# Two weights staged in spare activation buffers and narrowed earlier, and one matmul group moved ahead of another

## The chip, the cores and the metric

One core of a Trainium2 chip runs the whole program in one launch. The metric is the device time of one execution in microseconds (us). Before the change three runs gave 575.04, 575.33 and 576.16 us: a median of 575.33 us.

## What is computed

Three layers follow each other for a batch of 4 sequences of 576 positions. The first is attention with 8 heads of 64, a window of 128 and a linear bias. Its output, 512 wide, is the x of a gated layer:

```
h = gelu(x @ w_in)                       # 512 -> 1024
u, v = h[..., :512], h[..., 512:]
v_n = (v - mean(v)) / sqrt(var(v) + 1e-6) * g_ln
v_s = einsum('ts,bsd->btd', w_sg, v_n) + b_sg[None, :, None]     # w_sg is 576 x 576
y = x + (u * v_s) @ w_out                # w_out is 512 x 512
```

The third layer takes y through a second pair of weights with a convolution over positions and a gate. The weights w_in, w_out and those of the third layer arrive as 64-bit floats; w_sg arrives as 32-bit floats.

## The kernel before, in words

Every product is made from two-part operands: a value is split into a rounded part ("hi") and the rest ("lo"), and the three products hi\*hi, hi\*lo and lo\*hi are added up in PSUM (`mm`, L207). A 64-bit weight is first narrowed to 32 bits by five VectorE instructions (`narrowed`, L287: L301, L303, L304, L305, L306), then split by a copy (L216 on ScalarE or L219 on GpSimd) and a subtraction (L225).

The order of the work is written out as a list of steps (`_steps`, L55). A letter names the work, and the numbers say batch, half of the sequence and tile. Those that matter here, for batch 0:

- `V0.j` (`m_v`, L697): the psv product for positions j\*128 on, 12 matmuls, then gelu on ScalarE, statistics on VectorE, a power on GpSimd, a scaling and a split into vn. There are five.
- `U0.half.m` (`m_u`, L730): the psu product, 12 matmuls, and its gelu on ScalarE.
- `G0.half.m` (`m_sg`, L767): the pss product of w_sg and vn, 14 matmuls, read out by VectorE at L783. Its last two matmuls take the fifth piece of w_sg and the fifth vn.
- `W0.half.m` (`m_wo`, L788): the pso product with w_out, read out by VectorE into x.
- `L`, `M`, `C`, `E`, `N`, `T`, `A` for the next batch's attention: loads, scores with nine masking instructions on VectorE (L426), exponentials on ScalarE, scaling, transposes, and the product with the values.
- `g0` to `g4` (`w_sg_piece`, L343): one 128-row piece of w_sg is loaded, copied into its hi part and subtracted into its lo part.
- `ok.h` (`w_out_piece`, L349): one of eight pieces of w_out (128 rows by 256 columns) is loaded, narrowed and split.

The list is a priority and not the final order: a scheduler that runs at build time lays each engine's instructions in one fixed sequence. It takes the ready instruction that stands first in the list, by a timing model of its own, and it assigns buffers as they come free. `tc.keep_in_program_order` pins an instruction behind the one written just before it on the same engine. `later` (L326) keeps a load behind the last load of w_in on the queue of SyncE (SP), which issues nearly all loads.

Three sets of buffers matter. Tag "st" has four (`NST`): the keys and queries of a batch use them (`a_load`, L380), and before the change the pieces of w_sg and w_out too. Tag "x" has eight: batch 0 holds four of them for its attention output, and the other four are first wanted by batch 1. Tag "v" has three (`NV`): the v of a `V` step and the narrowed piece of w_out share them. The products psv, psu, pss and pso share two PSUM banks (`gps`).

The room in which the hi and lo parts of w_sg and w_out are kept holds inputs of batch 0's attention first (`z_room`, L567), so nothing can be written there until that attention is over.

Of the kernel before, what the change touches and what calls it, by code (L numbers as in the profile page):

```python
# [7 lines left out]
F32 = mybir.dt.float32  # L8
F32R = mybir.dt.float32r
# [30 lines left out]
SLACK = 6000.0  # L40

ON = {
    "clamp": "dve", "win hi": "act", "win lo": "pool", "w64 hi": "pool", "w64 lo": "pool", "w32 hi": "act pool", "w32 lo": "dve",
    "norm": "dve pool",
    "x hi": "act pool", "x lo": "dve", "x first hi": "act", "x first lo": "pool", "x late hi": "act", "x late lo": "dve", "vn first hi": "act", "vn first lo": "dve", "vn hi": "pool", "vn lo": "dve",
    "gate": "pool", "g hi": "act dve pool", "g lo": "dve pool", "x2 hi": "act pool", "x2 lo": "dve",
# [8 lines left out]
def _steps():  # L55


    def of(p):
        return f"{p // NP}.{p % NP}"

    def scores(p):
        return [f"C{of(p)}"]

    def weigh(p):
        return [f"E{of(p)}", f"N{of(p)}"]

# [12 lines left out]
    put_by = [f"a{i}.{c}" for i in (1, 0) for c in range(16)]
    s = """  # L80
        l0.0 k0 l1.0 k5 l2.0 l3.0 v0.0 v1.0 v2.0 v3.0 j1.0 j1.1 l0.1
        c0.0 e0.0 c1.0 e1.0 n0.0 c2.0 e2.0 t0.0 n1.0 c3.0 e3.0 l1.1 j1.2 j1.3 v0.1 i1.0 z0.0 X0.0.0 t1.0 n2.0 z1.0 X0.1.0
        l2.1 v1.1 i1.1 t2.0 n3.0 z2.0 X0.2.0 c0.1 e0.1 l3.1 j0.0 i1.2 t3.0 z3.0 X0.3.0 c1.1 e1.1 v2.1 i1.3 n0.1 c2.1 e2.1 j0.1 v3.1 j0.2 t0.1 n1.1 z0.1
        i0.0 c3.1 e3.1 j0.3 k4 V0.0 t1.1 n2.1 z1.1 i0.1 V0.1 t2.1 n3.1 z2.1 i0.2 U0.0.0 t3.1 z3.1 X0.0.1 U0.0.1
        X0.1.1 i0.3 U0.0.2 X0.2.1 X0.3.1 U0.0.3
    """.split()
    for b in range(B - 1):
        p = NP * (b + 1)
        V = [f"V{b}.{j}" for j in range(5)]
        U = [[f"U{b}.{half}.{m}" for m in range(4)] for half in range(2)]  # L90
        G = [[f"G{b}.{half}.{m}" for m in range(4)] for half in range(2)]
        W = [[f"W{b}.{half}.{m}" for m in range(4)] for half in range(2)]
        if b == 0:
            uv = V[2:4] + loads(p) + scores(p) + V[4:] + loads(p + 1) + U[1][:2] + scores(p + 1) + loads(p + 2) + U[1][2:] + scores(p + 2)
        else:
            uv = V[:2] + loads(p) + scores(p) + V[2:] + loads(p + 1) + scores(p + 1) + U[0] + loads(p + 2) + U[1][:1] + scores(p + 2) + U[1][1:]
        T, A = ([f"{x}{of(p + i)}" for i in range(4)] for x in "TA")
        gw = weigh(p) + G[0] + weigh(p + 1) + G[1][:1] + loads(p + 3) + T[:1] + W[0][:1] + A[:1] + halves(p)
        gw += weigh(p + 2) + W[0][1:2] + T[1:2] + W[0][2:] + A[1:2] + scores(p + 3) + halves(p + 1) + weigh(p + 3) + G[1][1:2] + T[2:3] + G[1][2:3]
        gw += A[2:3] + halves(p + 2) + G[1][3:] + T[3:] + W[1][:1] + A[3:] + halves(p + 3) + W[1][1:]  # L100
        if b == 0:
            s += weave(uv, [f"g{c}" for c in range(5)] + [f"o{k}.0" for k in range(4)]) + ["o0.1"] + gw[:2] + ["o1.1"] + gw[2:4] + ["o2.1"] + gw[4:6] + ["o3.1"] + gw[6:]
        else:
            now = put_by[10 * b - 10 : 10 * b]
            s += weave(uv, now[:4]) + weave(gw, now[4:])
    first = " ".join(s)
    n = [f"V3.{j}" for j in range(5)] + [f"U3.{half}.{m}" for half in range(2) for m in range(4)]
    n += [f"G3.0.{m}" for m in range(4)] + ["G3.1.0"] + [f"W3.0.{m}" for m in range(4)]
    n += [f"G3.1.{m}" for m in range(1, 4)] + [f"W3.1.{m}" for m in range(4)]

    for m in range(4):
        n[n.index(f"U3.{m % 2}.{m // 2 + 1}")] += f" w0.{m // 2}.{m % 2}"
    n[n.index("W3.0.3")] += " y0.0"
    n[n.index("G3.1.2")] += " y0.1"
# [20 lines left out]
def attention_gmlp_glu_kernel(  # L135
# [24 lines left out]
    def f(ap):  # L160
        return ap.bitcast(F32)
# [148 lines left out]
    def prep64(hi, lo, src, n, pool, tag, bufs, spool, stag, sbufs):  # L310
        a = narrowed(src, n, pool, tag, bufs, spool, stag, sbufs)
        split(hi, lo, a, "w64")

    def prep32(hi, lo, src, n, pool, tag, bufs):
        st = pool.tile([P, S], F32, tag=tag, name="wst", bufs=bufs)
        later(nc.sync.dma_start(st[:, :n], src))
        tc.keep_in_program_order(copy(hi, st[:, :n], engines=ON["w32 hi"]))
        tt(lo, st[:, :n], f(hi), ALU.subtract, ON["w32 lo"])
# [16 lines left out]
    def w_in_piece(half, k):  # L335
# [3 lines left out]
        else:  # L339
            sl = slice(k * P, (k + 1) * P)  # L340
            split(winh[:, :, sl], winl[:, :, sl], a.rearrange("p (k n) -> p k n", k=NK), "win")

    def w_sg_piece(c):  # L343
        if c == 0:
            kept["wsg"] = [w1pool.tile([P, 5, S], F32R, tag=f"wsg{i}", name=f"wsg{i}") for i in range(2)]
        wsg = kept["wsg"]
        prep32(wsg[0][:, c, :], wsg[1][:, c, :], w_sg[:, c, :], S, apool, "st", NST)

    def w_out_piece(k, half):  # L349
        if k == half == 0:  # L350
            kept["wo"] = [w1pool.tile([P, NK, DM], F32R, tag=f"wo{i}", name=f"wo{i}") for i in range(2)]
        wo = kept["wo"]
        sl = slice(half * 256, (half + 1) * 256)
        prep64(wo[0][:, k, sl], wo[1][:, k, sl], cols(w_out, k, half * 256, 256), 256, mpool, "v", NV, apool, "st", NST)

    p2pool = []

# [209 lines left out]
    def z_room(i):  # L567

        if i not in room:
            tag, n = (("wsg0", 5 * S), ("wsg1", 5 * S), ("wo0", NK * DM), ("wo1", NK * DM))[i]  # L570
            room[i] = w1pool.tile([P, n], F32, tag=tag, name="zin")
        return room[i]

# [214 lines left out]
    def m_wo(b, half, m):  # L788
        sl = HALF[half]
        n = sl.stop - sl.start  # L790
        cm = slice(m * P, (m + 1) * P)
        ps = gps.tile([P, 512], F32, tag="g", name="pso")
        o = ps[:, :n]
        wo = kept["wo"]
        i = 0
        for k in range(NK):
            hi, lo = gts[b, k, half]
            for w, a in ((wo[0], hi), (wo[1], hi), (wo[0], lo)):
                mm(o, w[:, k, cm], a, start=i == 0, stop=i == 3 * NK - 1)
# [249 lines left out]
```

## Time and profile before

| | us |
|---|---|
| median of three runs | 575.33 |
| the profiled execution | 575.59 |
| its span, first to last instruction | 573.7 |
| TensorE busy | 535.0 |
| VectorE busy | 381.1 |
| GpSimd busy | 266.3 |
| ScalarE busy | 246.3 |

The span is what the trace covers; 1.9 us of the profiled execution lie around it. Mean granted clock of TensorE was 0.979 of 2.4 GHz. The engines are named PE (TensorE), PEld (its weight loads), DVE (VectorE), ACT (ScalarE), POOL (GpSimd) and SP (the loads' queue). L207 is line 207 of the kernel. A square bracket in a timeline row gives the engine's idle time just before the row, and what ended it.

### The profile page before, as it was taken

Reading aid. Unit: us, or ns where it says so; the run is one execution under the profiler, and the core shown is the slowest. Engines: PE = TensorE matmul, PEld = TensorE weight load, DVE = VectorE, ACT = ScalarE, POOL = GpSimd, SP = SyncE. Lnnn points to the kernel's source line nnn. Section 1 sums busy time; section 2 is a strip of 40 time slices with the busy share of each in tenths; the row PEclk is TensorE's granted clock in tenths of the full one; section 3 lists DMA queues with packets and bytes.
Section 4 is the critical chain, followed back from the end, with each engine's and each line's share of the span. In section 5 each row is a group of like instructions: output and inputs, shape, how many; then the busy total and the mean of one; then the engine's idle time right before and its main releaser. Section 6 shows DMA issues by size and latency. Waiting matters only on the chain. (4 is left out here: it accounts for less than half of the span.)

```text
span 573.7 us, 11857 instructions
## 1 busy us (share of the span) xinstructions
PE 535.0 (93%) x4496; PEld 481.9 (84%) x4496; DVE 381.1 (66%) x974; ACT 246.3 (43%) x635; POOL 266.3 (46%) x410
## 2 busy tenths in 40 slices
PE   7867897899999899998999999998999999999997
PEld 6656687798789798888998889996898999898887
DVE  5978389964795886868876887678766533654300
ACT  6785147452328452239443311244545333434301
POOL 3653127931235362325362454468696354455500
PEclk9898897999999899999999999999999999999999
DMA  8971053443161457250735334630201210100011
GB/s 303 353 257 40 5 183 111 145 152 122 45 186 50 153 179 221 75 162 2 218 107 167 109 95 133 211 151 11 91 20 47 91 38 19 39 19 20 37 38 55
DMA packets 33208, 63.91 MB, mean 111 GB/s; under 512 B 3968, under 2 KB 13952, under 8 KB 33152
## 3 DMA queue, kind: packets, MB, share of 16 engines
q1 hardware_dynamic: 33008, 63.04, 33.2%
q8 instruction: 35, 0.57, 0.4%
q14 instruction: 21, 0.17, 0.1%
q10 hardware_dynamic: 144, 0.13, 0.1%
HBM read 48.47 MB, written 14.68 MB: 110 GB/s over the span
## 5 line engine op out<-in xcount | busy, mean ns | idle before, releaser
L207 PE MATMUL psg<-x2g,w 128*128 128x288 f32 x768 | 107.0, 296 | 1.2 <-DVE x2g L225 1.2
L207 PEld LDWEIGHTS psg<-x2g,w 128*128 128x128 f32 x768 | 104.5, 188 | 3.6 <-DVE x2g L225 2.1
L207 PE MATMUL psg<-wout,gh 128*128 128x512 f32 (+1 forms) x272 | 81.2, 383 | 1.8 <-ACT gh L216 1.8
L181 ACT ACTIVATE t<-t,st 128x192 f32<-128x192 f32 (+1 forms) x144 | 61.8, 432 | 21.4 <-DVE st L426 21.4
L207 PE MATMUL pss<-wsg,vn 128*128 128x256 f32 (+1 forms) x448 | 66.2, 306 | 3.6 <-DVE t L783 3.4
L207 PEld LDWEIGHTS pss<-wsg,vn 128*128 128x128 f32 x448 | 62.8, 197 | 4.6 <-DVE t L783 4.6
L207 PE MATMUL psu<-xh,win 128*128 128x256 f32 (+1 forms) x256 | 54.6, 306 | 8.1 <-ACT win L216 3.7
L909 DVE SCALAR_TENSOR_TENSOR cc<-hb,cw,cc 128x576 f32<-128x576 f32 x32 | 29.0, 908 | 49.1 <-POOL cc L236 49.1
L207 PEld LDWEIGHTS psg<-wout,gh 128*128 128x128 f32 x272 | 49.5, 188 | 12.2 <-ACT gh L216 2.4
L207 PE MATMUL pso<-gh,wo 128*128 128x256 f32 (+1 forms) x256 | 52.8, 301 | 3.0 <-DVE x L225 2.2
L207 PE MATMUL psv<-win,xh 128*128 128x512 f32 (+1 forms) x160 | 52.8, 410 | 2.7 <-ACT win L216 1.3
L207 PE MATMUL psg<-wout,gl 128*128 128x512 f32 (+1 forms) x136 | 52.1, 384 | 0.4 <-POOL gl L225 0.3
L236 POOL TENSOR_SCALAR t<-t,r 128x192 f32<-128x192 f32 (+1 forms) x86 | 40.5, 487 | 24.6 <-PE o L207 5.3
L207 PEld LDWEIGHTS psu<-xh,win 128*128 128x128 f32 x256 | 42.4, 193 | 10.1 <-ACT win L216 4.2
L225 POOL TENSOR_TENSOR gl<-gg,gh 128x512 fp32r<-128x512 f32 x32 | 46.7, 1459 | 1.0 <-ACT gh L216 1.0
L236 POOL TENSOR_SCALAR cc<-hb,cw 128x576 f32<-128x576 f32 x32 | 27.5, 862 | 39.8 <-ACT hb L905 39.8
L426 DVE CUSTOM_DVE_ANT_0 t<-sc,tab 128x192 f32<-128x192 f32 (+1 forms) x144 | 40.2, 335 | 6.4 <-PE sc L207 6.2
L207 PEld LDWEIGHTS pso<-gh,wo 128*128 128x128 f32 x256 | 40.2, 188 | 4.8 <-DVE x L225 2.7
L905 ACT ACTIVATE hb<-psg 128x576 f32<-128x576 f32 x32 | 20.7, 653 | 52.9 <-PE psg L207 51.4
L225 DVE TENSOR_TENSOR gg<-cc,hb 128x576 f32<-128x576 f32 x32 | 30.3, 952 | 18.0 <-ACT cc L181 17.6
L207 PE MATMUL pso<-gl,wo 128*128 128x256 f32 (+1 forms) x128 | 37.5, 301 | 3.9 <-DVE gl L225 3.9
L225 POOL TENSOR_TENSOR t<-t,u 128x256 f32<-128x256 f32 (+1 forms) x32 | 27.1, 852 | 28.1 <-DVE t L783 20.6
(89 smaller groups left out, 1048.7 us busy)
## 6 DMA issues: line engine op xcount, KB each, us to landing
V<-in_v_dram SPq DMA_DIRECT2D x12, 704.0 KB, 4.6
w<-in_w_out_dram SPq DMA_DIRECT2D x24, 256.0 KB, 3.0
x2s<-x2d SPq DMA_DIRECT2D x16, 288.0 KB, 3.0
w<-in_w_in_dram SPq DMA_DIRECT2D x8, 512.0 KB, 6.2
w<-in_w_in_dram SPq DMA_DIRECT2D x16, 256.0 KB, 2.8
wout<-w2d SPq DMA_DIRECT2D x8, 512.0 KB, 5.7
q<-in_q_dram SPq DMA_DIRECT2D x12, 320.0 KB, 3.8
out_dram<-ot SPq DMA_DIRECT2D x15, 256.0 KB, 2.0
```

Source lines behind the costliest of these rows:

```text
L181: ins = nc.scalar.activation(*args, **kw)
L207: return nc.tensor.matmul(out, lhsT, rhs, start=start, stop=stop, **kw)
L225: return (nc.vector if eng == "dve" else nc.gpsimd).tensor_tensor(dst, a, b, op=op)
L236: e.tensor_scalar(dst, src, col, 1.0, op0=ALU.mult, op1=ALU.mult)
L426: nc.vector.tensor_tensor_reduce(e, bank, table, scale=-SCALE, scalar=3e38, op0=ALU.add, op1=ALU.min, accum_out=mx)
L905: nc.scalar.activation(h[:, 1 : S + 1].rearrange("p (a n) -> p a n", a=2), ps[:, :, :288], AF.Relu)
L909: nc.vector.scalar_tensor_tensor(cc, h[:, 0:S], cw[:, 0, c : c + 1], cc, op0=ALU.mult, op1=ALU.add)
```

## The change

1. `w_sg` and `w_out` pieces are loaded into buffers of tag "x" and no longer into tag "st" (`staged` replaces the loads in `prep32` and `prep64`).
2. The steps `g` and `o` stand elsewhere in the list. Before, the `g` pieces and `o0.0` to `o3.0` were spread evenly over the work from `V0.2` to the third scores of batch 1, and `o0.1` to `o3.1` stood among the `G0` steps. Now all thirteen stand before the first `G0` step.
3. `V0.2` stands before `U0.0.3` and no longer behind it.
4. The copy into the hi part of a w_sg piece is no longer pinned. The hi copy of w_out goes to ScalarE (was GpSimd); the subtraction stays on GpSimd.
5. The hi and lo parts of w_out lie in one tile and no longer in two. Its size is that of the two together.

```diff
-        X0.1.1 i0.3 U0.0.2 X0.2.1 X0.3.1 U0.0.3
+        X0.1.1 i0.3 U0.0.2 X0.2.1 X0.3.1
...
-            uv = V[2:4] + loads(p) + scores(p) + V[4:] + loads(p + 1) + U[1][:2] + scores(p + 1) + loads(p + 2) + U[1][2:] + scores(p + 2)
+            uv = ["g0", V[2], "o0.0", U[0][3], "g1", "o0.1", V[3]] + loads(p) + ["o1.0"] + scores(p) + ["o1.1", V[4], "o2.0", "g2", "o2.1"]
+            uv += loads(p + 1) + U[1][:2] + ["g3", "o3.0"] + scores(p + 1) + ["g4", "o3.1"] + loads(p + 2) + U[1][2:] + scores(p + 2)
...
-            s += weave(uv, [f"g{c}" for c in range(5)] + [f"o{k}.0" for k in range(4)]) + ["o0.1"] + gw[:2] + ["o1.1"] + gw[2:4] + ["o2.1"] + gw[4:6] + ["o3.1"] + gw[6:]
+            s += uv + gw
...
+    def staged(src, dtype):
+        st = mpool.tile([P, S], dtype, tag="x", name="wst", bufs=8)[:, : src.shape[-1]]
+        later(nc.sync.dma_start(st, src))
+        return st
...
-        prep32(wsg[0][:, c, :], wsg[1][:, c, :], w_sg[:, c, :], S, apool, "st", NST)
+        hi, lo = (w[:, c, :] for w in kept["wsg"])
+        st = staged(w_sg[:, c, :], F32)
+        copy(hi, st, engines=ON["w32 hi"])
+        tt(lo, st, f(hi), ALU.subtract, ON["w32 lo"])
...
-        prep64(wo[0][:, k, sl], wo[1][:, k, sl], cols(w_out, k, half * 256, 256), 256, mpool, "v", NV, apool, "st", NST)
+        st = staged(cols(w_out, k, half * 256, 256), U32)
+        a = narrowed(st, 256, mpool, "v", NV, None, "x", 8)
+        split(kept["wo"][:, k, half, 0, :], kept["wo"][:, k, half, 1, :], a, "wo")
```

`ON["wo hi"]` is ScalarE and `ON["wo lo"]` GpSimd. `m_wo` and `z_room` address the one tile in place of the two.

## Rows read from the trace of the kernel before

**Rows 1.** The page: busy time by engine, and the masking group of VectorE.

```profile
PE 535.0 (93%) x4496; PEld 481.9 (84%) x4496; DVE 381.1 (66%) x974; ACT 246.3 (43%) x635; POOL 266.3 (46%) x410
...
L426 DVE CUSTOM_DVE_ANT_0 t<-sc,tab 128x192 f32<-128x192 f32 (+1 forms) x144 | 40.2, 335 | 6.4 <-PE sc L207 6.2
```

**Rows 2.** Stretches: length, busy PE, PEld, DVE, ACT, POOL (count), PEclk, DMA share, GB/s.

```profile
59.00:63.00 4.00, 4.00 (x12) 3.20 (x13) 0.00 (x0) 0.00 (x0) 1.17 (x1) 0.59 0.00 0
63.00:69.00 6.00, 5.47 (x46) 4.39 (x48) 1.43 (x3) 1.36 (x3) 0.74 (x2) 1.00 0.01 4
69.00:83.00 14.00, 13.41 (x145) 11.87 (x136) 12.41 (x49) 4.19 (x10) 4.07 (x8) 1.00 0.46 144
...
94.00:100.40 6.40, 6.40 (x28) 6.40 (x29) 5.65 (x14) 3.04 (x14) 6.40 (x12) 0.54 0.26 84
100.40:113.00 12.60, 11.85 (x194) 10.65 (x191) 12.43 (x27) 6.74 (x17) 12.60 (x22) 1.00 0.36 117
...
140.50:218.00 77.50, 74.15 (x768) 67.80 (x768) 58.88 (x200) 35.53 (x115) 30.50 (x57) 0.98 0.42 128
```

**Rows 3.** Who PE waited for from 57 to 140.5 us: total, times, longest.

```profile
PE pss L207 <- DVE t L783: 3.4, 1, 3.4
PE pso L207 <- DVE x L225: 2.2, 2, 1.7
PE psu L207 <- ACT win L216: 2.1, 1, 2.1
PE sc L207 <- DMA q<-in_q_dram: 1.0, 2, 0.6
PE psv L207 <- ACT u L181: 0.5, 1, 0.5
PE o L207 <- ACT ph L216: 0.5, 1, 0.5
PE pso L207 <- DVE t L783: 0.3, 1, 0.3
```

**Rows 4.** Timeline of PE: start, length, instruction, idle before.

```profile
58.87 0.58 PE L207 MATMUL psu<-xh,win 128*128 128x256 f32 x1 [2.07 <-ACT win L216]
...
82.75 1.82 PE L207 MATMUL pss<-wsg,vn 128*128 128x256 f32 x14
84.96 1.97 PE L207 MATMUL sc<-k,q 64*64 64x128 f32 x46 [0.40 <-DMA q<-in_q_dram]
86.64 3.92 PE L207 MATMUL pss<-wsg,vn 128*128 128x256 f32 x28
93.96 6.61 PE L207 MATMUL pss<-wsg,vn 128*128 128x256 f32 x28 [3.40 <-DVE t L783]
```

**Rows 5.** Timeline of DVE.

```profile
57.48 0.69 DVE L306 SCALAR_TENSOR_TENSOR wa<-w,wa 128x512 uint32<-128x512 uint32 x1
65.91 0.70 DVE L721 BATCH_NORM_STATS2 bs<-v 128x6 f32<-128x512 f32 x1 [7.75 <-ACT v L181]
...
83.02 0.76 DVE L225 TENSOR_TENSOR wsg<-wst,wsg 128x576 fp32r<-128x576 f32 x1 [0.44 <-POOL wsg L219]
83.70 0.29 DVE L301 TENSOR_SCALAR wa<-w 128x256 uint32<-128x256 uint32 x1
...
85.14 0.43 DVE L306 SCALAR_TENSOR_TENSOR wa<-w,wa 128x256 uint32<-128x256 uint32 x1
...
88.83 0.84 DVE L301 TENSOR_SCALAR wa<-w 128x256 uint32<-128x256 uint32 x1
```

**Rows 6.** A stretch, instructions on tile wa alone: length, DVE, ACT, POOL, clock, DMA.

```profile
83.70:118.00 34.30, 17.87 (x40) 0.00 (x0) 9.63 (x16) 0.90 0.42 140
```

**Rows 7.** Timeline of POOL.

```profile
88.66 0.86 POOL L225 TENSOR_TENSOR t<-t,u 128x256 f32<-128x256 f32 x1 [1.74 <-DVE t L783]
```

**Rows 8.** Timeline of ACT.

```profile
65.29 0.59 ACT L181 ACTIVATE v<-psv 128x512 f32<-128x512 f32 x1
```

**Rows 9.** What SP's queue waited for from 30 to 120 us.

```profile
SPq L316 <- PE sc L207: 30.4, 1, 30.4
```

More of the change, by code (lines that the diff above doesn't have):

```diff
@@ L42 @@
 ON = {
-    "clamp": "dve", "win hi": "act", "win lo": "pool", "w64 hi": "pool", "w64 lo": "pool", "w32 hi": "act pool", "w32 lo": "dve",
+    "clamp": "dve", "win hi": "act", "win lo": "pool", "w64 hi": "pool", "w64 lo": "pool", "w32 hi": "act pool", "wo hi": "act", "wo lo": "pool", "w32 lo": "dve",
     "norm": "dve pool",
@@ L308, in narrowed @@
         return f(a)
[L310 to L318, printed above, removed]
     def cols(w, k, c0, n):
@@ L345, in w_sg_piece @@
             kept["wsg"] = [w1pool.tile([P, 5, S], F32R, tag=f"wsg{i}", name=f"wsg{i}") for i in range(2)]
-        wsg = kept["wsg"]
-        prep32(wsg[0][:, c, :], wsg[1][:, c, :], w_sg[:, c, :], S, apool, "st", NST)
+        hi, lo = (w[:, c, :] for w in kept["wsg"])
+        st = staged(w_sg[:, c, :], F32)
+        copy(hi, st, engines=ON["w32 hi"])
+        tt(lo, st, f(hi), ALU.subtract, ON["w32 lo"])
     def w_out_piece(k, half):
         if k == half == 0:
-            kept["wo"] = [w1pool.tile([P, NK, DM], F32R, tag=f"wo{i}", name=f"wo{i}") for i in range(2)]
-        wo = kept["wo"]
-        sl = slice(half * 256, (half + 1) * 256)
-        prep64(wo[0][:, k, sl], wo[1][:, k, sl], cols(w_out, k, half * 256, 256), 256, mpool, "v", NV, apool, "st", NST)
+            kept["wo"] = w1pool.tile([P, NK, 2, 2, 256], F32R, tag="wo", name="wo")
+        st = staged(cols(w_out, k, half * 256, 256), U32)
+        a = narrowed(st, 256, mpool, "v", NV, None, "x", 8)
+        split(kept["wo"][:, k, half, 0, :], kept["wo"][:, k, half, 1, :], a, "wo")
     p2pool = []
@@ L569, in z_room @@
         if i not in room:
-            tag, n = (("wsg0", 5 * S), ("wsg1", 5 * S), ("wo0", NK * DM), ("wo1", NK * DM))[i]
+            tag, n = (("wsg0", 5 * S), ("wsg1", 5 * S), ("wo", 2 * NK * DM))[i]
             room[i] = w1pool.tile([P, n], F32, tag=tag, name="zin")
@@ L593, in z_vload @@
         if half == 0:
-            V = z_room(3)[:, m * 512 : m * 512 + 512]
+            V = z_room(2)[:, 2048 + m * 512 : 2560 + m * 512]
             s["V"] = {c: V[:, c * P : (c + 1) * P] for c in range(2)}
@@ L790, in m_wo @@
         n = sl.stop - sl.start
-        cm = slice(m * P, (m + 1) * P)
         ps = gps.tile([P, 512], F32, tag="g", name="pso")
         o = ps[:, :n]
-        wo = kept["wo"]
+        wo = kept["wo"][:, :, m // 2, :, m % 2 * P : m % 2 * P + P]
         i = 0
@@ L797, in m_wo @@
             hi, lo = gts[b, k, half]
-            for w, a in ((wo[0], hi), (wo[1], hi), (wo[0], lo)):
-                mm(o, w[:, k, cm], a, start=i == 0, stop=i == 3 * NK - 1)
+            for w, a in ((0, hi), (1, hi), (0, lo)):
+                mm(o, wo[:, k, w, :], a, start=i == 0, stop=i == 3 * NK - 1)
                 i += 1
```

## The prediction

> **What bounds the kernel now.** I read four views, from the whole to the spot. The page says that PE is busy for 535.0 us and DVE for 381.1 [rows 1]: PE sets the time wherever it doesn't wait, so I looked for the stretch in which it waits or runs slowly. The table of stretches shows it [rows 2]. Batch 1 needs 77.5 us for all of its work on x at a mean clock of 0.98, with PE busy 74.15 us. Batch 0's stage around the change has two poor places: at 59 to 63 us the clock is 0.59, and at 94 to 100.4 us it is 0.54. Both follow a wait of PE, which the timeline gives [rows 4]: 2.07 us before the first matmul of U0.0.3 (for the last piece of w_in), and 3.40 us before the fourth group of pss, which waits until DVE has read out an earlier one. The list of waits adds the small ones: 1.0 us for loads of q, 0.5 us for a PSUM bank, 2.2 us for DVE's read-out of pso [rows 3].
>
> The reason for the 3.40 us stands on the other engines. DVE has nothing to do from the end of w_in's last narrowing (57.48 + 0.69 = 58.17 us) to 65.91 us, and then a queue: three V steps, two sets of masks, w_sg, and from 83.70 us on the narrowing of w_out, in which the read-outs of pss stand in line [rows 5]. Narrowing takes 17.87 us of DVE and 9.63 us of POOL between 83.7 and 118 us [rows 6], where DVE is busy 12.43 of 12.60 us and POOL all of it (100.4 to 113 us) [rows 2]. The loads were the cause: SP's queue stood 30.4 us at one load of w_sg until the scores of batch 1 gave back a buffer [rows 9].
>
> **V0.2 ahead of U0.0.3.** V0.2 needs no part of w_in that is late; it needs a PSUM bank, which the gelu of an earlier psu frees. The nearest row for such a wait is the 0.5 us for "ACT u" [rows 3], so 2.07 becomes 0.5: 1.6 us earlier. The slow clock behind it: 4.00 us at 0.59 is 3.3 us at half rate, 1.6 us lost [rows 2]. The 1.7 us wait for pso [rows 3] lies in no slow stretch, so I take the loss as gone; the bounds are 0 and 1.6. V0.2's gelu (65.29 us before, behind that of U0.0.3 [rows 8]) then comes some 5 us earlier. With it goes the 0.5 us bank wait. Tag "st" no longer holds weights, so the keys and queries of the second pair can be loaded with the first: the 1.0 us for q goes [rows 3]. PE thus reaches its first pss at 82.75 - 1.6 - 1.6 - 0.5 - 1.0 = 78.0 us, not 82.75 [rows 4]. The scores of C1.2 (1.97 us [rows 4]) can be drawn ahead: 80.0 us.
>
> **The narrowing ahead of the first pss.** pss can't end before the last lo part of w_sg, at 83.02 + 0.76 = 83.78 us before [rows 5]. DVE's work up to there, from 58.17 us, was 1.43 + 12.41 + 0.76 = 14.6 us [rows 2, 5]. In front of it now stand seven of the eight narrowings; the eighth, o3.1, is pinned behind g4's subtraction. One narrowing is 83.70 to 85.57 us where POOL is quiet: 1.87 us [rows 5]. The mean of all was 17.87 / 8 = 2.23 us [rows 6]. An upper end is 4.2 us: five instructions at the 0.84 us that one took [rows 5] while POOL ran a two-input instruction (from 88.66 us [rows 7]). I take 1.87, because POOL was busy only 4.8 of the 20 us from 63 to 83 [rows 2] and gets only eight subtractions and less than before to copy. One us more goes to waits inside V0.2, before other work can fill DVE. The last lo part then lands at 58.17 + 14.6 + 7 x 1.87 + 1.0 = 86.9 us, later than before. Without the idle us, and with one set of masks (nine at 0.335, 3.0 us [rows 1]) behind it, it would be 82.9; at 2.23 each, 89.4.
>
> So PE arrives at 80 us, does the twelve matmuls of the first pss that don't need the last piece, and waits some 5 us in all. The first group ends at 87.2 us. Four more groups follow. Behind 3.40 us of waiting, 28 matmuls took 6.61 us; at full clock 3.92 [rows 4]. I take one such pair of groups slow and one fast: 10.5 us, end at 97.7. Before, the same five groups and C1.2 ended at 100.4 [rows 2]: **2.7 us gained**, bounds -0.2 (last lo at 89.4) to +9.4 (last lo at 82.9, both pairs fast, 83.2 + 7.8 = 91.0).
>
> The 3.40 us for the read-out go, since the narrowing that stood among the masks is over by then; next in line is the split of the gated product (POOL), which has less beside it.
>
> **Behind 100.4 us.** DVE and POOL lose what was left of w_out. PE's waits there were 1.7 us (the longer one for pso's read-out), 0.3 and 0.5 us [rows 3]: **2.5 us gained**; bounds 0, if other work lines up in their place, and 3.0.
>
> **What costs nothing.** The hi copies of w_out go to ACT, which was busy 5.6 of 20 us from 63 to 83 [rows 2]; eight of some 0.4 us are hidden there. If they aren't, a gelu and so a PSUM bank is late by 0.4 us. The loads of thirteen pieces carry the same bytes; four land in the spare buffers before 58 us, and the other nine wait on SP for a buffer, with loads of keys, queries and values queued behind them. Those have their own buffers and are due only at the scores. A wait for a buffer of tag "v" holds a gelu on ACT, and behind it a PSUM bank; three pieces and v's share the three, so I count up to 1 us, inside the bounds above. One tile for w_out changes no matmul's shape: nothing. Batches 1 to 3 and the last layer keep their work: nothing, they only start earlier.
>
> **Sum.** -2.7 - 2.5 = -5.2 us against the profiled 575.59 (span 573.7 and 1.9 around it): 570.4. That execution lies 0.26 us above the median, so 570.1 against 575.33.
>
> **Rivals.**
>
> *The narrowing stretches, and it is slower.* POOL's subtractions for w_out run beside DVE's next narrowing. If a piece costs more than p in 58.17 + 15.6 + 7p + 0.3 + 10.5 = 100.4 + 2.5, that is 2.6 us, the change loses. At 3.2 us, midway between the mean and the upper end, the last lo part lands at 96.2 us, the five groups end at 107.0, and the time is 575.3 + 6.6 - 2.5 = 579.4. For it: the 0.84 against 0.29 us of one and the same instruction [rows 5]. Against it: POOL's low share from 63 to 83 us [rows 2]. The Trainium skill, page "GPSIMD Engine Reference", section "Specifications", says that POOL shares its SBUF interfaces with VectorE and contends with VectorE instructions of two inputs or of a two-port mode. The trace agrees for one pair, 0.84 us beside 0.86 us of POOL; by that rule the price depends on what POOL does in the new place, and the forecast stands only while it is nearly idle. Chance 0.16.
>
> *The wait only moves.* The last lo part comes at 89.4 us, PE waits nine us before the first pss, starts at half clock, and the waits behind 100.4 us are filled by others: 575.1. Chance 0.12.
>
> *DVE is ahead.* The last lo part at 82.9 us, no slow clock, and the 2.5 us: -9.4 - 2.5 gives 563.4 against the median; with one pair of groups slow (2.7 us), 566.1. Chance 0.20.
>
> That the change doesn't do what it says is hardly possible here: the buffers of "x" are free until batch 1's attention, and the loads no longer share with the keys. That leaves 0.52 for the forecast, whose own range is 563.4 to 575.1.
>
> **How the numbers follow.** About 0.2%, 1.15 us, is what a measurement of this kernel can tell from no change: 574.2 to 576.5 is the same. Of the forecast's 0.52 I put 0.50 below 574.2; with the 0.20 and a twentieth from the rival that only moves the wait: faster 0.75. Same: 0.10. Slower: 0.15. The range leaves out the far ends of the first and the third rival: 563.5 to 576.5.
>
> **What would show it.** Right: V0.2's first psv at some 57.3 us with the clock near 1 from 59 to 63; no gap of 7.75 us on DVE; the last lo part of w_sg at 85 to 88 us and a wait of PE of some 5 us for it; no 3.40 us wait for L783; w_out done before 95 us; batch 1's first psv at some 135 us in place of 140.5. Wrong: narrowing over 2.6 us a piece; gelus that wait for a buffer; a slow clock through all of pss; or a gain up to 100 us that is gone at 140.

## The result and the profile after

The changed kernel takes **579.85 us** (median of 14 runs, 576.37 to 581.50) against 575.71 us for the kernel before in the same runs (575.04 to 578.04): a ratio of 1.0058, 95% interval 1.0040 to 1.0076. It is slower by 4.1 us by the medians and 3.3 us by the ratio; 570.1 was predicted. Its profiled execution took 577.27 us (span 575.2), which is 2.6 us under its own median, so the profile shows less of the loss than the runs do.

The lines of the changed kernel are shifted: L207 of before is L208, L225 is L226, L783 is L781. Busy time on the page says nothing of the loss; PE is busy for less than before [rows 1]:

```profile
PE 533.9 (93%) x4496; PEld 482.1 (84%) x4496; DVE 376.4 (65%) x968; ACT 249.1 (43%) x642; POOL 265.7 (46%) x409
```

The same stretches as in [rows 2]:

```profile
59.00:63.00 4.00, 3.43 (x16) 2.59 (x15) 1.78 (x4) 1.22 (x2) 1.28 (x1) 1.00 0.00 2
63.00:69.00 6.00, 6.00 (x68) 4.81 (x67) 4.38 (x18) 1.90 (x4) 0.85 (x3) 1.00 0.02 5
69.00:83.00 14.00, 10.65 (x88) 8.93 (x87) 10.58 (x40) 4.16 (x9) 5.67 (x9) 0.88 0.44 144
...
94.00:100.40 6.40, 5.87 (x35) 5.87 (x36) 4.29 (x11) 6.40 (x30) 6.40 (x13) 0.73 0.01 3
100.40:113.00 12.60, 11.51 (x166) 10.64 (x164) 6.69 (x11) 7.41 (x21) 12.49 (x25) 1.00 0.25 77
...
140.50:218.00 77.50, 72.10 (x746) 66.05 (x746) 58.23 (x198) 35.24 (x114) 30.92 (x57) 0.98 0.41 125
```

Three things stand out. At 59 to 63 us the clock is 1.00 and no longer 0.59. From 69 to 83 us PE is busy 10.65 us where it was 13.41: a new hole. And from 140.5 to 218 us, where the list of steps is unchanged, PE is busy 72.10 us instead of 74.15: a second hole, behind the change.

Who PE waits for from 57 to 140.5 us, as in [rows 3]:

```profile
PE psu L208 <- ACT v L182: 3.3, 1, 3.3
PE pss L208 <- DVE t L781: 2.6, 1, 2.6
```

The first is new, the second was 3.4 us. PE's timeline has their places, as in [rows 4] (the first row is V0.2's psv, which stood behind a wait of 2.07 us and now starts 0.53 us after the last psu):

```profile
58.38 0.73 PE L208 MATMUL psv<-win,xh 128*128 128x512 f32 x2 [0.53 <-ACT u L182]
...
76.85 0.56 PE L208 MATMUL psu<-xh,win 128*128 128x320 f32 x2 [3.35 <-ACT v L182]
...
90.00 1.93 PE L208 MATMUL pss<-wsg,vn 128*128 128x256 f32 x14 [0.58 <-ACT wsg L217]
94.53 7.15 PE L208 MATMUL pss<-wsg,vn 128*128 128x256 f32 x42 [2.61 <-DVE t L781]
```

**The first hole.** The matmul at 76.85 us needs a PSUM bank, which ACT frees with V0.4's gelu. ACT's timeline shows that gelu waiting for DVE (second row), and DVE's why: V0.3's scaling and its vn, which frees the v buffer, stand behind the subtraction of the third piece of w_sg, and that waits 1.53 us for its hi copy, and the copy 2.46 us for the load. ACT:

```profile
72.82 0.67 ACT L217 CAST wsg<-wst 128x576 fp32r<-128x576 f32 x1 [2.46 <-DMA wst<-in_w_sg_dram]
...
76.21 0.59 ACT L182 ACTIVATE v<-psv 64x512 f32<-64x512 f32 x1 [0.82 <-DVE vn L226]
```

DVE, the same execution, as in [rows 5]:

```profile
53.53 3.30 DVE L226 TENSOR_TENSOR wsg<-wst,wsg 128x576 fp32r<-128x576 f32 x2 [0.23 <-PE o L208]
...
73.52 0.76 DVE L226 TENSOR_TENSOR wsg<-wst,wsg 128x576 fp32r<-128x576 f32 x1 [1.53 <-ACT wsg L217]
74.20 0.54 DVE L724 TENSOR_SCALAR v<-v,ba,rs 128x512 f32<-128x512 f32 x1
...
75.42 0.69 DVE L226 TENSOR_TENSOR vn<-v,vn 128x512 fp32r<-128x512 f32 x1 [0.68 <-ACT vn L217]
...
90.00 0.75 DVE L226 TENSOR_TENSOR wsg<-wst,wsg 128x576 fp32r<-128x576 f32 x1
...
93.29 0.80 DVE L302 TENSOR_SCALAR wa<-wst 128x256 uint32<-128x256 uint32 x1 [0.68 <-POOL wo L226]
```

So two buffer sets meet. The ring of three v buffers (buffers used in turn) is shared by v and w_out's narrowed pieces, and a gelu stands in line for it; and the loads stand in line for a staging buffer. In the list of SP's waits from 52 to 92 us (total, times, longest) the staging loads of L336 wait 36.2 us with DVE as the releaser:

```profile
SPq L336 <- DVE wsg L226: 15.5, 3, 12.6
SPq L336 <- DVE st L424: 11.4, 1, 11.4
SPq L336 <- DVE wa L307: 9.3, 3, 4.6
```

**The second hole** is one wait behind 140.5 us, in batch 1. There pT is a transposed piece of the attention's weights in PSUM, ph its copy in SBUF, o their product with the values, and w_out2 the second weight of the third layer. PE's row after, and then the row of the kernel before at the same instructions:

```profile
195.65 2.04 PE L208 MATMUL o<-ph,V 128*64 128x64 f32 x52 [2.53 <-issue]
```

```profile
195.35 2.05 PE L207 MATMUL o<-ph,V 128*64 128x64 f32 x52 [0.57 <-ACT ph L216]
```

DVE there, after and before. The kernel runs the same instructions, in another order: the narrowing of a piece of w_out2 (L304 to L307) now stands ahead of the copies ph<-pT for which PE waits, and not behind them. On PE and ACT the order of batch 1 is the same in both. PE starts these matmuls 56.8 us after the batch's first psv, where it was 54.8.

```profile
192.09 0.28 DVE L302 TENSOR_SCALAR wa<-w 128x256 uint32<-128x256 uint32 x1
192.41 0.29 DVE L304 TENSOR_SCALAR wa<-wa 128x256 f32<-128x256 f32 x1
192.74 0.29 DVE L305 TENSOR_SCALAR wa<-wa 128x256 uint32<-128x256 uint32 x1
193.07 0.43 DVE L306 SCALAR_TENSOR_TENSOR wa<-w,wa 128x256 uint32<-128x256 uint32 x1
193.53 0.42 DVE L307 SCALAR_TENSOR_TENSOR wa<-w,wa 128x256 uint32<-128x256 uint32 x1
193.87 0.68 DVE L219 COPY ph<-pT 128x512 f32<-128x512 f32 x1
...
194.87 0.68 DVE L219 COPY ph<-pT 128x512 f32<-128x512 f32 x1
```

```profile
193.76 0.29 DVE L301 TENSOR_SCALAR wa<-w 128x256 uint32<-128x256 uint32 x1
193.97 1.28 DVE L218 COPY ph<-pT 128x512 f32<-128x512 f32 x2
...
195.56 0.29 DVE L303 TENSOR_SCALAR wa<-wa 128x256 f32<-128x256 f32 x1
```

The list of steps for batch 1 is the same in both kernels. The scheduler that lays the instructions at build time took another choice there, and again in the last layer: before, it drew four matmuls of the first output product ahead of the last psg matmuls on x (192 of those come first after, 144 before; psg are the products of the third layer). PE's waits from 347 us on change with it: 2.6, 0.8 and 0.4 us (for gl on POOL, gh on ACT, x2g on DVE) where they were 0.3, 1.8 and 1.2. That is 0.5 us more. The other 0.6 us by which the last layer is longer are busy time of PE, 220.9 us instead of 220.3: behind those waits its granted clock is at the lower level, where it was at the full one (after, then before):

```profile
402.00:405.50 3.50, 3.05 (x14) 2.71 (x13) 2.45 (x2) 1.46 (x3) 2.05 (x4) 0.51 0.18 43
```

```profile
402.00:405.50 3.50, 3.29 (x20) 2.87 (x21) 3.18 (x4) 2.17 (x4) 3.50 (x4) 1.00 0.08 19
```

### The profile page after: what moved, and what is told of

Same layout as the page of the kernel before. It is cut to its first block, busy times and chain, and to the rows that moved or that the text cites. A ratio compares the mean times of both kernels' runs of the same rounds, so it can differ in the third digit from the quotient of the medians.

```text
span 575.2 us, 11859 instructions
## 1 busy us (share of the span) xinstructions
PE 533.9 (93%) x4496; PEld 482.1 (84%) x4496; DVE 376.4 (65%) x968; ACT 249.1 (43%) x642; POOL 265.7 (46%) x409
## 5 line engine op out<-in xcount | busy, mean ns | idle before, releaser
L208 PE MATMUL psg<-x2g,w 128*128 128x288 f32 x768 | 107.6, 298 | 0.4 <-DVE x2g L226 0.4
L208 PEld LDWEIGHTS psg<-x2g,w 128*128 128x128 f32 x768 | 105.6, 190 | 2.3 <-DVE x2g L226 0.8
L208 PE MATMUL psg<-wout,gh 128*128 128x512 f32 (+1 forms) x272 | 81.3, 383 | 0.8 <-ACT gh L217 0.8
L208 PE MATMUL pss<-wsg,vn 128*128 128x256 f32 (+1 forms) x448 | 65.0, 303 | 3.3 <-DVE t L781 2.6
L208 PEld LDWEIGHTS pss<-wsg,vn 128*128 128x128 f32 x448 | 61.7, 194 | 4.3 <-DVE t L781 3.5
L208 PE MATMUL psu<-xh,win 128*128 128x256 f32 (+1 forms) x256 | 54.3, 305 | 9.6 <-ACT v L182 4.1
L906 DVE SCALAR_TENSOR_TENSOR cc<-hb,cw,cc 128x576 f32<-128x576 f32 x32 | 27.0, 847 | 48.7 <-POOL cc L237 48.7
L208 PEld LDWEIGHTS psg<-wout,gh 128*128 128x128 f32 x272 | 49.4, 188 | 10.8 <-ACT gh L217 1.1
L208 PE MATMUL psv<-win,xh 128*128 128x512 f32 (+1 forms) x160 | 51.7, 400 | 3.8 <-POOL win L226 1.4
L208 PE MATMUL psg<-wout,gl 128*128 128x512 f32 (+1 forms) x136 | 52.4, 385 | 2.6 <-POOL gl L226 2.6
L208 PE MATMUL pso<-gh,wo 128*128 128x256 f32 (+1 forms) x256 | 52.5, 300 | 0.6 <-ACT gh L217 0.5
L208 PEld LDWEIGHTS psu<-xh,win 128*128 128x128 f32 x256 | 42.0, 191 | 12.1 <-ACT v L182 4.6
L237 POOL TENSOR_SCALAR t<-t,r 128x192 f32<-128x192 f32 (+1 forms) x93 | 42.7, 476 | 14.3 <-DVE r L650 6.7
L237 POOL TENSOR_SCALAR cc<-hb,cw 128x576 f32<-128x576 f32 x32 | 29.0, 908 | 41.9 <-ACT hb L902 41.9
L226 POOL TENSOR_TENSOR gl<-gg,gh 128x512 fp32r<-128x512 f32 x32 | 46.5, 1454 | 1.3 <-ACT gh L217 1.3
L226 DVE TENSOR_TENSOR gg<-cc,hb 128x576 f32<-128x576 f32 x32 | 32.4, 1019 | 17.3 <-ACT cc L182 17.3
L208 PEld LDWEIGHTS pso<-gh,wo 128*128 128x128 f32 x256 | 40.2, 188 | 1.8 <-ACT gh L217 0.9
L208 PE MATMUL pso<-gl,wo 128*128 128x256 f32 (+1 forms) x128 | 37.5, 300 | 3.9 <-DVE gl L226 3.9
L226 POOL TENSOR_TENSOR t<-t,u 128x256 f32<-128x256 f32 (+1 forms) x32 | 26.8, 845 | 26.0 <-DVE t L781 13.9
```

Of the source, the lines that this page charges most:

```text
L208: return nc.tensor.matmul(out, lhsT, rhs, start=start, stop=stop, **kw)
L226: return (nc.vector if eng == "dve" else nc.gpsimd).tensor_tensor(dst, a, b, op=op)
L237: e.tensor_scalar(dst, src, col, 1.0, op0=ALU.mult, op1=ALU.mult)
L906: nc.vector.scalar_tensor_tensor(cc, h[:, 0:S], cw[:, 0, c : c + 1], cc, op0=ALU.mult, op1=ALU.add)
```

## The experiments

The table is read from the PE timeline of each profiled execution: where V0.2's psv and batch 1's first psv start, how long batches 1 and 2 take (first psv to first psv), the way from batch 3's first psv to the first psg, and from there to the end of the span. The kernel before ran beside each group of runs; its median is in the last column.

| kernel | V0.2 | batch 1 at | batch 1 | batch 2 | to psg | last | median | before |
|---|---|---|---|---|---|---|---|---|
| before | 59.25 | 140.55 | 81.8 | 81.9 | 42.8 | 226.6 | | 575.71 |
| after | 58.38 | 138.88 | **83.9** | 81.9 | 42.8 | **227.7** | 579.85 | 575.71 |
| after, again | 60.59 | 142.30 | **83.3** | 81.9 | 44.4 | **227.6** | 580.86 | 575.89 |
| V0.2 first alone | 58.55 | 140.37 | **85.5** | **85.3** | 44.4 | 226.6 | 583.16 | 575.89 |
| own ring | 57.72 | 136.30 | 81.9 | 81.9 | 42.8 | 226.6 | 573.16 | 575.89 |
| old places | 63.93 | 146.63 | 81.9 | 82.0 | 42.8 | 226.5 | 585.45 | 575.89 |
| ph first | 58.62 | 139.12 | 82.2 | 81.9 | 44.6 | **227.6** | 577.89 | 575.94 |
| narrowing first | 61.80 | 140.95 | **82.2** | 81.9 | 42.8 | **229.2** | 578.23 | 575.94 |
| own ring, w_sg first | 60.77 | 140.52 | 81.9 | 81.9 | 44.5 | 226.5 | 574.45 | 575.94 |
| own ring, g0 later | 58.21 | 137.99 | 81.9 | 82.0 | 42.8 | 226.6 | 576.37 | 576.42 |
| own ring, last layer | 58.46 | 140.71 | 81.9 | 81.9 | 42.8 | **230.0** | 577.44 | 576.42 |
| own ring again | 58.10 | 137.04 | 81.8 | 81.9 | 42.8 | 226.7 | 571.46 | 575.95 |
| own ring, w_sg sooner | 57.52 | 138.34 | 81.8 | 81.9 | 42.8 | 226.6 | 574.81 | 575.95 |

Bold marks the places that the build laid in another order than in the kernel before. Of the columns, "to psg" is 44.4 to 44.6 us in some executions and 42.8 in others, also of one and the same kernel (after: 42.8, again: 44.4), at a lower granted clock.

**The changed kernel again** (no edit).

> The changed kernel once more, for a second trace of it. Its first trace (577.27 us) had batch 1's first psv at 138.88 us, 1.67 earlier than before, and lost 2.1 us in batch 1 and 1.1 us in the last layer; its runs spread from 576.4 to 581.5 us. Theory A (the stage itself is sound, the loss lies behind it): first psv of batch 1 again at 138 to 140 us and the missing us behind 140. Theory B (the stage varies from run to run with the clock): first psv of batch 1 moves by 2 us or more between the two traces, with the granted clock of 69 to 101 us. Ratio to before 1.004 to 1.008 by both.

580.86 us, ratio 1.0078 (1.0049 to 1.0107): the loss stands in other runs. The later loss stands too, 83.3 us for batch 1 and 227.6 for the last layer. But theory B holds for the stage: batch 1 starts 1.75 us later than before instead of 1.67 earlier. Of the 3.4 us between the two traces 2.2 lie ahead of V0.2, where the granted clock was 0.90 (0 to 30 us) and 0.86 (30 to 57 us) instead of 1.00 and 0.87; 1.2 lie behind it. So what the stage gains is not in every execution.

**V0.2 ahead of U0.0.3 alone**, in the kernel before:

```diff
-        X0.1.1 i0.3 U0.0.2 X0.2.1 X0.3.1 U0.0.3
+        X0.1.1 i0.3 U0.0.2 X0.2.1 X0.3.1
...
-            uv = V[2:4] + loads(p) + ...
+            uv = [V[2], U[0][3], V[3]] + loads(p) + ...
```

> The kernel before with one part of the change alone: V0.2 ahead of U0.0.3. Theory (as predicted): the 2.07 us wait for w_in becomes some 0.5, the clock from 59 to 63 us stays near 1, 2 to 3.5 us gained at 83 us; of it 0 to 3 us are left at batch 1's first psv (137.5 to 140.5), since the read-out of pss then waits as before. Rival: the gain is eaten at once by the 3.40 us wait, and batch 1's first psv stands at 140 to 141; time within 0.2% of before.

583.16 us, ratio 1.0122 (1.0097 to 1.0148): one swapped step costs 7 us. Up to batch 1 the rival is right: it starts at 140.37 us as before. Neither theory has the rest: batches 1 and 2 take 3.6 and 3.4 us more, and there the build has put w_out2's narrowing ahead of the copies ph<-pT, in both batches. PE's waits from 140 to 310 us:

```profile
PE o L207 <- issue: 3.9, 1, 3.9
PE o L207 <- DVE ph L218: 3.8, 1, 3.8
```

In batch 1 every engine has the changed kernel's order, yet that order cost 2.1 us there and 3.6 here. PE starts the matmuls of o 56.8 us into the batch in both (here at 197.19 us, there at 195.65):

```profile
197.19 2.78 PE L207 MATMUL o<-ph,V 128*64 128x64 f32 x52 [3.91 <-issue]
```

What differs is where a stretch at the lower clock fell: here behind the wait, where it delays all that follows (first row), in the changed kernel ahead of it, where the wait took it up (second row).

```profile
198.30:201.70 3.40, 3.40 (x37) 3.28 (x33) 0.92 (x2) 1.03 (x3) 0.46 (x1) 0.50 0.52 153
```

```profile
187.00:190.40 3.40, 3.33 (x48) 2.87 (x49) 3.33 (x12) 1.07 (x3) 2.14 (x5) 0.50 0.34 84
```

So 2.0 us are the later ph, and the other 1.6 us fit 3.40 us at half the clock.

**Its own ring for w_out's narrowed pieces**: two buffers of their own in place of the tag "v".

```diff
-        a = narrowed(st, 256, mpool, "v", NV, None, "x", 8)
+        a = narrowed(st, 256, apool, "wa", 2, None, "x", 8)
```

> The changed kernel with the narrowed piece of w_out in two buffers of its own (tag wa) and no longer in the three that the v of the V steps uses. Theory C (the v ring is the cause in the stage): the 3.35 us wait of psu for the gelu of V0.4 and the 2.61 us wait of pss for a read-out both shrink to under 1 us, and batch 1's first psv comes 3 to 5 us earlier, at 134 to 136 us. Theory D (the staging rotation is the cause: the third piece of w_sg is loaded only when a staging buffer comes free, and its subtraction stands on DVE ahead of V0.3's scaling): the 3.35 us wait stays at 2.5 us or more.

573.16 us, ratio 0.9957 (0.9935 to 0.9979): faster than both kernels. The wait of 3.35 us is 0.6 and PE is busy 13.45 of 14 us from 69 to 83, by theory C. The subtraction of w_sg's third piece stands on DVE ahead of V0.3's scaling as before, and waits as long for its copy; only the gelu no longer hangs on it:

```profile
72.89 0.76 DVE L226 TENSOR_TENSOR wsg<-wst,wsg 128x576 fp32r<-128x576 f32 x1 [1.56 <-ACT wsg L217]
```

Theory C promised more than came: the wait for the read-out is 1.6 us and not under 1, and batch 1 starts at 136.30 us, 2.6 us earlier and not 3 to 5. By this edit the build also lays all later work as before the change, so the run joins two effects, which the next runs take apart. What is left in the stage, with waits for w_sg's pieces that are new:

```profile
PE pss L208 <- ACT wsg L217: 2.4, 1, 2.4
PE pss L208 <- DVE t L781: 1.6, 1, 1.6
PE pss L208 <- DVE wsg L226: 1.5, 2, 1.1
```

**The new staging with the steps at their old places in the list** (the old `uv`, the old `weave` line, and U0.0.3 back in the first block).

> The changed kernel with the steps of w_sg, w_out, V0.2 and U0.0.3 at their old places in the list: staging in tag x, hi of w_out on ACT, the unpinned copy and the one tile of w_out stay. Theory (the new places cost, the staging doesn't): as fast as before or up to 2 us faster (573.5 to 576), since the loads no longer wait for the scores. Rival (staging or the moved copies cost by themselves): 577 us or more, and batch 1's first psv later than 140.5.

585.45 us, ratio 1.0154 (1.0118 to 1.0189): the rival. All later work is as long as before; the loss is ahead of batch 1, which starts 6.1 us later (the profiled execution took 581.67 us, the least of the six, so the median has some 4 us more that no trace shows). The spare buffers let the pieces of w_sg load before w_in is finished, and on DVE all five of their subtractions stand ahead of w_in's last narrowing, which starts 4.7 us later than the 55.38 us of before:

```profile
54.73 3.87 DVE L225 TENSOR_TENSOR wsg<-wst,wsg 128x576 fp32r<-128x576 f32 x4 [0.98 <-PE o L207]
58.52 0.94 DVE L225 TENSOR_TENSOR xl<-x,xh 128x320 fp32r<-128x320 f32 x1
59.39 0.75 DVE L225 TENSOR_TENSOR wsg<-wst,wsg 128x576 fp32r<-128x576 f32 x1
60.06 0.41 DVE L301 TENSOR_SCALAR wa<-w 128x512 uint32<-128x512 uint32 x1
```

PE then waits 5.2 us for that piece. So the new staging loses at the old places in the list. The run doesn't part the spare buffers from the copy that is no longer pinned, and it doesn't show that the moved steps cost nothing.

**The order of batch 1 restored** in the changed kernel, by two order-only dependencies:

```diff
+        clamped.append(...)                      # in narrowed: its clamp instruction
...
             p1 = turned([whole(t, 1, i) for i in range(4)])
+            if (b, m) == (2, 1):
+                for x in copies[-2:]:
+                    tc.add_manual_dep(clamped[-1].ins, x.ins.name, follow, reason="order")
```

> The changed kernel with one order restored in the work of batch 1: the four instructions on DVE that narrow the sixth piece of w_out2 (from the clamp on) are laid behind the two copies ph<-pT of the same row of heads, as before the change, instead of ahead of them. The stage up to 138.9 us stays as in the changed kernel, and so does the order of the last layer. Theory (part of the loss is this other order of DVE's queue, which keeps PE waiting for ph): the stretch from batch 1's first psv to batch 2's falls from 83.9 us to 81.9 to 82.4, the waits o<-issue 2.5 and o<-DVE ph 2.0 behind 140 us go, and the median is 1.5 to 2 us under the changed kernel's 579.85, at 578.0 (577.0 to 579.2). Rival (those 2 us are a matter of the granted clock or of the run): the stretch stays at 83.3 to 83.9, and the median at 579.9.

577.89 us, ratio 1.0034 (1.0012 to 1.0055), where 578.0 was expected. Only DVE's rows at this place are laid differently from the changed kernel. Batch 1 takes 82.2 us instead of 83.9, and PE's wait of 2.53 us is:

```profile
194.28 2.04 PE L208 MATMUL o<-ph,V 128*64 128x64 f32 x52 [0.97 <-ACT ph L217]
```

The stage and the last layer are as in the changed kernel. About half of the loss goes with one place in DVE's queue. (The other wait that was to go, 2.0 us for ph in batch 2, stays, here as in the changed kernel, and costs nothing: PE starts those matmuls 54.8 us into batch 2, as in the kernel before, which waited 0.6 us there, behind 3.4 us at a clock of 0.50.)

**The opposite order imposed on the kernel before**, by a dependency of the first copy on the last narrowing instruction.

> The kernel before with the opposite order imposed at the same place in batch 1: the first of the two copies ph<-pT on DVE is laid behind the whole narrowing of that piece of w_out2. Nothing ahead of 140 us differs from the kernel before; the build then also lays the last layer in the order that the changed kernel has. Theory (the order costs, with no part of the change in the kernel): the stretch from batch 1's first psv to batch 2's rises from 81.8 us to 83.9 or more, the last layer from 226.6 to 227.7, and the median is 3 us over the kernel before, 578.7 (577.3 to 581). Rival (the order costs nothing by itself): 81.8 and 226.6, median 575.7.

578.23 us, ratio 1.0035 (1.0014 to 1.0056): slower without any part of the change, as expected, but not by the expected places. Batch 1 took only 0.4 us more, because the forced order also put two read-outs of pso ahead of the copies and PE found other matmuls:

```profile
195.80 0.50 PE L207 MATMUL pso<-gh,wo 128*128 128x256 f32 x2 [1.94 <-DVE x L225]
```

The last layer, which the build then laid as in the changed kernel, took 229.2 us, with the granted clock at 0.50 from 402.6 to 409.4 us. So the price of an order depends on what else is laid around it; "narrowing ahead of ph" alone is not worth 2 us everywhere.

**Own ring, all of w_sg first**: `g0 V0.2 g1 U0.0.3 g2 g3 V0.3 ... g4 ... o0.0 V0.4 o0.1 ...`, the eight w_out pieces behind.

> The changed kernel with w_out's narrowed pieces in a ring of their own (as in the run with its own ring, 573.16) and the order of the pieces turned: the five pieces of w_sg first, one or two to a step of psv or psu, then the eight of w_out. The later work is laid as in the kernel before. Theory (what is left of waits at the first pss is the staging rotation: a w_sg piece loads only when a w_out piece before it has left its buffer): the waits of pss for wsg, 2.4 on ACT and 1.5 on DVE, go, the first pss starts by 81 instead of 82.45, the first pT of the next attention by 95.5 instead of 97.9, and the median is 2 to 3 us under 573.16, at 570.7 (569.5 to 572.5). Rival 1 (w_out then comes too late, and pso waits for wo, or the read-outs of pss stand behind its narrowing): the stage up to batch 1 is no shorter than 78.6 us, and the median 573 to 575. Rival 2 (PE was not held by the pieces of w_sg but by DVE as a whole): within 1 us of 573.16.

574.45 us, ratio 0.9977 (0.9959 to 0.9996; one of the twelve executions took 1776.38 us and is not in the ratio): the first rival, by its time and by the stage, 79.8 us from V0.2 to batch 1. The first pss starts at 85.47 us, not by 81. The waits for wsg are gone, and others stand in their place: 2.9 us for the read-out of pss, 2.0 for x, 1.6 for w_in's last piece, 1.2 for gl.

**Own ring, g0 behind V0.2** in the list.

> The changed kernel with w_out's narrowed pieces in their own ring (573.16 in its run) and one step moved: the first piece of w_sg stands behind V0.2 in the list instead of ahead of it. Batches 1 and 2 and the last layer are laid as in the kernel before. Theory (the early subtraction on DVE, 1.65 us a piece beside POOL, delays the last split of X0.3.1 and the last narrowing of w_in, but PE is not waiting for them): within 1 us of 573.2, batch 1 and batch 2 at 81.9 us each, the last layer at 226.5. Rival (those 1.8 us stand on PE's path): the stretch up to V0.3 is 1.5 us shorter and the median is at 571.7.

576.37 us, ratio 0.9985 (0.9962 to 1.0008): neither. It is 3 us slower than expected, and the new wait is 3.6 us of psu for w_in. The profiled execution, 573.06 us, is the second fastest of twelve and shows 1.7 of these 3 us, in the start of batch 1.

**Own ring, only the last layer in the changed kernel's order** (w_sg spread between V0.2 and V0.4, w_out mostly behind).

> The changed kernel with the own ring and another order of the same steps (w_sg's pieces spread between V0.2 and V0.4, w_out's mostly behind them). By the build, batches 1 and 2 are then laid as in the kernel before, and only the last layer in the order of the changed kernel. Theory (each other order has its own price): batch 1 and batch 2 at 81.9 us each, the last layer at 227.6 instead of 226.5, median 1.1 us over 573.2 plus or minus 1 for the stage, 574.3 (573 to 575.5). Rival (the 1.1 us of the last layer are the granted clock of single runs): the last layer at 226.5.

577.44 us, ratio 1.0020 (1.0004 to 1.0036). Batches 1 and 2 are as expected; the last layer took 230.0 us. The median lies above the expected range, but the stage is longer as well (batch 1 starts at 140.71 us, with 4.4 us of psu waiting for w_in), so the median doesn't separate the two. What can be said is by the table: the last layer takes 227.6 to 230.0 us in the five executions with this order, and 226.5 to 226.7 in the eight with the other. The clock has a part in it: in all five it falls to 0.50 some 54 to 58 us into the last layer, behind the waits, for 3.4 us (6.8 in narrowing first), and in none of the eight. The 230.0 us also hold a wait of 1.1 us of pso for gh, at 362.80 us, that the changed kernel doesn't have.

**Own ring, all three places in the other order** (w_out's first pieces ahead of w_sg's).

> The changed kernel with the own ring and a third order of the same steps (w_out's first pieces ahead of w_sg's). By the build, batch 1 and batch 2 then have the narrowing of a w_out2 piece ahead of the copies ph<-pT, and the last layer has the changed kernel's order: three places instead of two. Theory (the later order, and not the stage, makes most of the changed kernel's loss): batch 1 at 83.9 us and batch 2 at 83.9 to 85.4, the last layer at 227.7, median 573.2 + 2 + 2 to 3.5 + 1.1, so 578.3 to 579.8, slower than the kernel before though the ring is apart. Rival (with the ring apart the kernel stands at 573 to 574 whatever the later order): 573.5.

585.17 us, ratio 1.0126 (1.0079 to 1.0174): with the ring apart, the kernel is slower than before by more than the orders were expected to cost. Its profiled execution, 592.12 us, is the longest of six that spread from 580.02, so it isn't in the table and its lengths carry little weight. In it batches 1 and 2 take 85.4 and 85.3 us, as in V0.2 first alone, but batch 1 starts at 146.09 us: this list of steps also lengthens the stage, so the run doesn't price the orders.

**Own ring, once more.**

> The run with w_out's narrowed pieces in their own ring once more, on another chip, to see whether 573.16 stands. Theory (ring apart, and by that also the later work laid as before the change): 573.2 (572.5 to 574.5), under the kernel before by 2 to 3 us in the same runs; batch 1 and batch 2 at 81.9 us each, the last layer at 226.5. Rival (a lucky set of runs): within 1 us of the kernel before.

571.46 us, ratio 0.9941 (0.9920 to 0.9962): it stands, on another chip, and is 1 us below the expected range.

**Own ring, g1, g3 and g4 one to four places sooner.**

> The same kernel with w_sg's second, fourth and fifth pieces one to four places sooner in the list, and w_out's pieces between them later; the later work is laid as in the kernel before. Theory (the waits of the first pss for wsg, 2.4 on ACT and 1.5 on DVE, come from the staging buffers, which a w_sg piece shares with the w_out pieces listed ahead of it): those two waits fall under 1 us together, and the median is 1 to 2 us under the run with its own ring, at 571.7 (570.5 to 573.2). Rival (DVE has the same work to do by the first pso wherever it stands, as when all of w_sg came first): another wait, of pso or of the read-outs, takes their place, and the median is 573 to 575.

574.81 us, ratio 0.9976 (0.9957 to 0.9995): the rival's time, with other waits than it named. No wait for wsg is left, but psu waits 2.9 us for w_in, because the early pieces of w_out now share DVE's and ACT's queues with w_in's last one. Its last copy on ACT stands behind w_out's and a gelu, at 62.76 us, where it ran at 59.32 us in the run with its own ring:

```profile
61.96 0.41 ACT L217 CAST wo<-wa 128x256 fp32r<-128x256 f32 x1 [3.49 <-DVE wa L307]
62.27 0.59 ACT L182 ACTIVATE v<-psv 128x512 f32<-128x512 f32 x1
62.76 0.61 ACT L217 CAST win<-wa 128x512 fp32r<-128x512 f32 x1
```

## Why the prediction was wrong

Its direction was wrong: 570.4 us was forecast for the profiled execution, and 577.27 came. Of these 6.9 us, 3.8 stand in the first term. The five groups of pss end at 101.68 us (94.53 + 7.15) where they ended at 100.57 (93.96 + 6.61): 1.1 us lost in place of 2.7 gained. The second term came: from there to batch 1 it is 37.2 us instead of 40.0, 2.8 gained for 2.5. And 3.2 us were lost behind batch 1's start, where the sum has nothing.

The step that turned the sign is "Batches 1 to 3 and the last layer keep their work: nothing, they only start earlier". They keep their work but not its order, though I had described the scheduler myself: a changed stage gives it other buffers and other times in its model, and it lays later instructions differently. In the profiled execution that cost 2.1 us in batch 1 and 1.1 us in the last layer, 3.2 us, which alone turns the 1.67 us by which batch 1 starts earlier into the 1.5 us by which the span is longer. Restoring batch 1's order took back some 2 us of the median (by the ratios 0.24% against the changed kernel, 0.44% against its second run), and one swapped step with that order in two batches cost 7 us, part of it by the clock.

The step that failed in the first term is the size of "a wait for a buffer of tag "v" ... up to 1 us": it was 3.35 us, with a mean clock of 0.88 from 69 to 83 us around it, and PE came to its first pss at 87.44 us, not at 80.0. The wait was so long since the v buffer hung on a vn that stood behind a w_sg subtraction, which stood behind a load, which stood behind a staging buffer. I had costed the nine loads that wait on SP at nothing, because the keys and queries behind them were not due. What was due was the w_sg piece itself, and everything laid behind it on DVE. Of the signs of being wrong that the prediction names, this one came: a gelu that waits for a buffer.

The other terms, in their order:

- **V0.2 first:** right in mechanism. 2.07 us became 0.53, and the clock from 59 to 63 us is 1.00. But V0.2 started at 58.38 us, not 57.3, and the low clock came back around the new hole (0.88 from 69 to 83 us), so the second term of 1.6 us was not kept.
- **The narrowing:** right in size. Tile wa on DVE from 57 to 102 us is 15.94 us; less the 2.65 us of w_in's last piece (five rows from 57.15 to 59.94 us) that is 13.3 us, 1.66 us for each of eight pieces where I took 1.87:

```profile
57.00:102.00 45.00, 15.94 (x45) 3.52 (x9) 6.49 (x8) 0.92 0.29 93
```

- **The last lo part:** I summed DVE's work and put it at 86.9 us (82.9 to 89.4); it ended at 90.75. DVE was not the bound of that sum: from 69 to 83 us it was busy 10.58 of 14 us, and it waited for hi copies and loads. A sum of work is a lower bound where the queue has waits in it. PE's wait for it, put at some 5 us, is only 0.58 (at 90.00 us), because PE itself came late. And the bound written as -0.2 us, for the last lo part at 89.4, comes out at +0.2 by its own sum (89.4 + 0.3 + 10.5 against 100.4).
- **The 3.40 us for the read-out** fell only to 2.61: the read-outs stood behind the last w_out piece (93.29 us), which waited for POOL.
- **Behind 100.4 us:** right, as said above. PE is busy 37.9 of the 39 us from 101 to 140 us, where it was 36.0.
- **The rivals:** the narrowing did not stretch. The time is near the 579.4 us of the first rival, but by coincidence: its mechanism is not what happened. The Trainium skill, "GPSIMD Engine Reference", section "Specifications", lets VectorE and POOL contend for their SBUF interfaces; the trace agrees for w_sg's first two subtractions, 1.65 us each at 53.53 us beside POOL's two of 3.04 us together, where one alone takes 0.75 us. They put w_in's last narrowing at 57.15 us where it was 55.38, and no wait of PE in the changed kernel was for it. The prediction's own pair, 0.84 beside 0.86 us, is a VectorE instruction of one input; whether it ran in a two-port mode, as that rule wants, no row shows.

**What the cause is, and how far it is shown.** The v ring is shown by the kernel with its own ring, twice: the 3.35 us go, and from V0.2 to batch 1 it is 78.6 and 78.9 us instead of 80.5 and 81.7. The order in batch 1 is shown by the run that restores it. The last layer's price, some 1.1 us, goes with the order in the thirteen executions of the table, but only 0.5 us of it stands in PE's list of waits, the rest in the clock behind them, and no run restored that order in the changed kernel. That this order brings the low clock is not shown. Nor is the price of the small parts of the change that no run took alone: w_out's hi copies on ScalarE, its one tile, and the copy that is no longer pinned. Why the scheduler chooses as it does stays open. So does the last part of the loss, between the profiled 577.27 and the median 579.85 us: the repeated profile has 2.2 us of it ahead of V0.2 and 1.6 us between batch 3 and the last layer, both at a low clock.

## What to carry to other kernels

Where a scheduler lays the instructions, an edit reaches as far as the program does: compare the laid order of every engine, also far behind the edit, before crediting or blaming the edit itself. Look for staged weights that share a ring with an activation on the critical path: here two small buffers apart, with the later order that they brought, turned 4 to 5 us of loss into 2.7 and 4.5 us of gain. That gain hung on the list of steps as well: with five other lists the same ring stood at 574.45 to 585.17 us. Judge a wait by when the engine goes on, not by how long it stood. And an engine's work added up gives the earliest end, not the end, once its operands come from buffers that rotate.

## What was not expected of the hardware

Two executions with the same instructions in the same order up to 57 us differ in the granted clock and by 2.55 us: the kernel before had a granted clock of 0.94 from 0 to 30 us and 0.94 from 30 to 57 us and reached V0.2 at 59.25 us; the kernel with the imposed order, which differs from it only behind 140 us, had 0.89 and 0.86 and reached it at 61.80. So a profile of one execution can hide or feign a stage's gain of 2 us; the lengths of batches 1 and 2, 81.8 to 82.0 us in the eight executions with the old order in both, are far steadier to compare.

They are so steady although the clock in them is not. In the kernel before it was 0.50 from 188.6 to 192.0 us, and PE then waited 0.57 us for ph (195.35 us, 54.8 into the batch). With w_sg sooner it was 1.00 through the whole of batch 1, and PE waited 1.89 us:

```profile
193.11 2.04 PE L208 MATMUL o<-ph,V 128*64 128x64 f32 x52 [1.89 <-issue]
```

That is 54.8 us into the batch again: a slow stretch ahead of such a wait cost nothing, while one behind it cost some 1.6 us in V0.2 first alone.
